# Selective attention and SwiGLU in one kernel: the last 64 queries of batch 0 among the feed-forward products, its causal mask by a matmul, single PSUM banks, loads one behind another

## The chip, the cores and the metric

The kernel runs on one core of one Trainium2 chip. The metric is the time of one execution on the device in microseconds, here 382.61 as the median of three runs (382.60 to 382.98). The profile that is read below is of one further execution of 383.17 us, whose span from the first to the last instruction is 381.3 us.

## The reference: what is computed

Attention with a positional bias over 8 batches, 8 heads, 576 positions and head width 64, and then a SwiGLU feed-forward block over the 4608 tokens that come out of it (width 512, inner width 1536). All inputs are float32.

```python
scores = q @ k.T / sqrt(64)
cum    = cumsum(maximum(s, 0))                      # per batch and head
bias   = -(cum[:, None] - cum[None, :])
scores = where(causal, -1e9, scores + minimum(bias, 0))
attn   = softmax(scores)                            # rows end at the diagonal
x      = (attn @ v) as [tokens, heads * 64]
out    = (silu(x @ w_gate) * (x @ w_val)) @ w_out
```

576 positions are four blocks of 128 and a tail of 64. The 4608 tokens are nine feed-forward tiles of 512, so a tile isn't a batch: tile 0 needs the first 512 queries of batch 0 and no more.

## The kernel before

All products are in bf16. A score product takes k as the stationary operand and q as the moving one, so a block of scores has keys on the partitions; the bias is in it by four further rows of both operands (the tile HL, copied by small transfers into kq). The exponential writes bf16 into `pt`; the causal triangle is then set to zero by an affine select on GpSimd; the product with v (with a column of ones for the sum) gives the output and its divisor; four or five transposes per pair of heads bring it into `XT`, from which the feed-forward tiles read. All instructions of an engine run in the order in which the program lists them. Batch 0's attention runs ahead of everything (`first_batch`), and the attention of the later batches is pumped in small pieces among the feed-forward products.

The parts that matter here; `take` gives the PSUM bank that was released longest ago:

```python
    CHUNKS = [
        [(0, 0, 128), (1, 128, 256), (2, 256, 384), (3, 384, 512)],
        [(0, 128, 576), (3, 512, 576)],
        [(1, 256, 576), (2, 384, 576)],
        [(4, 512, 576)],
    ]
    CHUNK_PT = [1088, 576, 0, 512]
# ... (cut)
        bank = {}
        for i in range(2):
            bank["w", i] = psa.tile([128, 1024], FP32, name=f"wide{i}")
        for i in range(4):
            bank["s", i] = psa.tile([128, 512], FP32, name=f"one{i}")
        released = {key: i - 8 for i, key in enumerate(bank)}
        clock = [0]
        OPEN = 1 << 40

        def take(kind="s"):
            b = min((x for x in bank if x[0] == kind), key=lambda x: released[x])
            assert released[b] < OPEN
            released[b] = OPEN
            return b

        def give(b):
            clock[0] += 1
            released[b] = clock[0]
# ... (cut)
        def score_piece(bh, ci):
            hb, hh = divmod(bh, HB)
            pair = bh < H
            if ci == 0:
                pts[bh] = PTP[0].tile(
                [128, PTW], BF16, tag="pt", bufs=PTP["bufs"], name="pt"
            )
            pt = pts[bh]
            r, e = divmod(hh, 2)
            T = KQ[hb % 2][r]
            if pair:
                if ci % 2 == 0:
                    bs = take("w")
                    scs[bh] = bs
                else:
                    bs = scs[bh]
                base = (512, 0, 0, 512)[ci]
            else:
                bs = take()
                base = 0
            o = base
            n = sum(hi - lo for _, lo, hi in CHUNKS[ci])
            sc = view(bs, 1024 if pair else 512)
            for (tj, lo, hi) in CHUNKS[ci]:
                w = hi - lo
                nc.tensor.matmul(
                    sc[:, o : o + w],
                    T[:, 1, e * S + 128 * tj : e * S + 128 * (tj + 1)],
                    T[:, 0, e * S + lo : e * S + hi],
                    start=True,
                    stop=True,
                )
                o += w
            if not pair or ci % 2 == 1:
                if pair:
                    c0, W = ((576, 1024), (0, 576))[ci // 2]
                else:
                    c0, W = CHUNK_PT[ci], n
                nc.scalar.activation(pt[:, c0 : c0 + W], sc[:, 0:W], AF.Exp, scale=0.125)
                give(bs)
            if ci == (1 if pair else 0):
                nc.gpsimd.affine_select(
                    pt[:, 1088:1600], pt[:, 1088:1600], pattern=[[0, 4], [1, 128]],
                    compare_op=ALU.is_ge, fill=zreg, base=0, channel_multiplier=-1,
                )
            if ci == 3:
                nc.gpsimd.affine_select(
                    pt[:, 512:576], pt[:, 512:576], pattern=[[1, 64]],
                    compare_op=ALU.is_ge, fill=zreg, base=0, channel_multiplier=-1,
                )
# ... (cut)
        def gate_value(tt, hps, sus):
            xt = XT[:, :, (tt % 3) * TT : (tt % 3 + 1) * TT]
            for ft in range(NFT):
                j, f0 = divmod(ft * 128, WCH)
                gbs = take()
                pg = view(gbs, TT)
                for c in range(4):
                    nc.tensor.matmul(
                        pg, WG[j][:, c, f0 : f0 + 128], xt[:, c, :],
                        start=(c == 0), stop=(c == 3),
                    )
                th = hpool.tile([128, TT], BF16, tag="th", name="th")
                nc.scalar.activation(th, pg, AF.Tanh, scale=0.5)
                pp = hpool.tile([128, TT], BF16, tag="pp", name="pp")
                nc.vector.scalar_tensor_tensor(
                    pp, in0=th, scalar=1.0, in1=pg, op0=ALU.add, op1=ALU.mult
                )
                give(gbs)
                yield 1.0
# ... (cut)
        cast_half(0, "k", 0, nc.scalar)
        cast_half(0, "q", 0, nc.scalar)
        aug(0, SP4)
        load_v(0, range(5))
        load_qk(2)
        for nm in ("k", "q"):
            for g in range(2):
                pe_transpose_half(0, nm, g, 0)
        pe_out(0, "k", 0, 0, nc.scalar)
        pe_out(0, "k", 1, 0, nc.scalar)
        pe_out(0, "q", 0, 0, nc.vector)
        pe_out(0, "q", 1, 0, nc.vector)
        cast_half(0, "k", 1, nc.scalar)
        cast_half(0, "q", 1, nc.gpsimd)
        aug(1, GP4)
        for nm, eng in (("k", nc.scalar), ("q", nc.vector)):
            for g in range(2):
                pe_transpose_half(0, nm, g, 1)
                pe_out(0, nm, g, 1, eng)
        cast_one(1, "k", nc.vector)
        cast_one(1, "q", nc.vector)
# ... (cut)
        def first_batch():
            wq = {1: (("g", 0), ("v", 0)), 4: (("g", 1),), 5: (("v", 1),)}
            tail = {
                6: ("a0", "a1"),
                7: ("a2", "a3", "a4", "x0", "a5", "x1", "a6", "a7", "x2", "w6", "x3", "w8"),
            }
            for h in range(H):
                for ci in range(4):
                    score_piece(h, ci)
                for w in wq.get(h, ()):
                    w_load(*w)
                if h == 1:
                    order = [(nm, g) for g in range(2) for nm in ("k", "q")]
                    for nm, g in order:
                        pe_transpose(1, nm, g)
                    for r in range(2):
                        for nm, g in order:
                            pe_out(1, nm, g, r, nc.vector)
                    for c in range(3, 5):
                        cast_v(0, c, nc.vector)
                if h == 2:
                    for c in range(3):
                        cast_v(0, c, nc.gpsimd)
                if h == 3:
                    aug(2, SP4)
                if h == 7:
                    aug(3, SP4)
                    load_qk(3)
                    load_v(1, range(5))
                    load_qk(4)
                    cast_one(2, "k", nc.gpsimd)
                    cast_one(2, "q", nc.gpsimd)
                    load_qk(5)
                    w_load("o", 0)
                    w_load("o", 1)
                for what in tail.get(h, ()):
                    i = int(what[1:])
                    if what[0] == "a":
                        av_piece(i, range(NCH))
                        av_out(i)
                    elif what[0] == "x":
                        x_pe(i, nc.scalar)
                    else:
                        keep_warm(i)

        first_batch()
        second_psum()
# ... (cut)
        hook = {
            1: [lambda: prep_one(2, 0)],
            2: [lambda: prep_one(2, 1)],
            3: [lambda: prep_one(2, 2)],
            4: [lambda: prep_one(2, 3)],
            6: [lambda: cast_one(3, "k", nc.gpsimd), lambda: cast_one(3, "q", nc.gpsimd)],
        }
        for tt in range(NTT):
            lo = H * (tt + 1) + LAGS[tt]
            hi = min(H * (tt + 2) + LAGS[tt + 1], BH + 2)
            span = 36 if tt < FIRST7 else 34.5
            if hi == BH + 2:
                span = 30
            n0 = 6 if tt == 0 else 0
            n = 0
            todo = {FIRST7 - 1: W_SUMS, FIRST7: W_DIFFS}.get(tt, [])
            for i, cost in enumerate(ffn_items(tt)):
                n += cost
                if todo and (i >= 24 if tt < FIRST7 else i % 4 == 2):
                    weight_op(*todo.pop(0))
                if i >= 2 * NFT or i % 4 == 1:
                    do_later(1)
                for f in hook.pop(n, ()):
                    f()
                pump(lo + (hi - lo) * min(1.0, max(0, n - n0) / (span - n0)))
```

The softmax here doesn't subtract the row's maximum and nothing guards it: scores larger than these inputs give would overflow.

## Time and profile before

| What | Value |
|---|---|
| median time | 382.61 us (3 runs, 382.60 to 382.98) |
| span in the profile | 381.3 us, 8674 instructions |
| VectorE, ScalarE, GpSimd busy | 289.6, 242.7 and 205.9 us |
| gate and value products, 128x512, x432 each | 110.9 and 110.8 us busy |
| tanh on ScalarE, 128x512, x108 | 64.7 us, 599 ns each |
| select 128x512 and 128x64 on GpSimd, x64 each | 41.8 and 16.7 us, 653 and 261 ns each |
| DMA, whole run | 64.22 MB in 100729 packets, 81888 of them under 512 B |

In the tables of the profile "busy" counts pipelined matmuls by modelled ends, so two successive busy times can overlap: four products of 512 columns are shown as 1.03 us, while the next group begins 0.86 us after them. "L375" is line 375 of the kernel file, "[0.57 <-DMA ...]" an idle time of the engine and what ended it.

### The profile page before, as it was taken

The page shows a single profiled execution, that of the slowest core. Times are in us where ns is not written, and L with a number is a line of the kernel's source. Part 1 is how long each engine was busy: PE and PEld are TensorE (multiplying, and loading weights), DVE is VectorE, ACT ScalarE, POOL GpSimd, SP SyncE. Part 2 cuts the span into 40 slices and gives each one's busy share as a digit, 9 for nine tenths or more (in the row PEclk, how much of TensorE's full clock was granted, in tenths as well). Part 3 has the DMA queues.
Part 4 walks back from the last instruction along what each step waited for, and adds up shares of the span by engine and source line. Part 5 has one row for each costly group of instructions (what it writes and reads, how often), then busy time and mean ns, then how long its engine had stood idle before and what let it go on. Part 6 is the DMA issues. An engine that isn't in the chain of part 4 may idle for free. (4 is left out here: it accounts for less than half of the span.)

```text
span 381.3 us, 8674 instructions
## 1 busy us (share of the span) xinstructions
PE 363.5 (95%) x3246; PEld 230.5 (60%) x3246; DVE 289.6 (76%) x577; ACT 242.7 (64%) x459; POOL 205.9 (54%) x326
## 2 busy tenths in 40 slices
PE   3779999998999999999999999999999999999995
PEld 3666556655555555865586558655875575476464
DVE  8666787456895799868986899589958866975983
ACT  8586788676977786578767876697455523323321
POOL 6684357545364636595458647775665426315220
PEclk9999999999999999999999999999999999999999
DMA  7999999997477998498739965987223213002003
GB/s 234 197 253 263 198 242 268 348 259 162 163 167 246 236 285 220 105 287 216 194 114 285 270 149 158 252 179 166 37 80 101 32 19 127 0 2 97 14 2 110
DMA packets 100729, 64.22 MB, mean 168 GB/s; under 512 B 81888, under 2 KB 85824, under 8 KB 100688
## 3 DMA queue, kind: packets, MB, share of 16 engines
q1 hardware_dynamic: 91248, 46.15, 48.6%
q0 software_dynamic: 9440, 17.53, 17.7%
q8 instruction: 25, 0.41, 0.4%
q14 instruction: 16, 0.13, 0.1%
HBM read 37.90 MB, written 19.86 MB: 151 GB/s over the span
## 5 line engine op out<-in xcount | busy, mean ns | idle before, releaser
L388 ACT ACTIVATE pt<-bank 128x512 bf16<-128x512 f32 x224 | 106.7, 506 | 26.5 <-PE bank L375 18.3
L626 PE MATMUL bank<-XT,wg 128*128 128x512 bf16 x432 | 110.9, 379 | 0.6 <-DVE pp L633 0.2
L641 PE MATMUL bank<-XT,wv 128*128 128x512 bf16 x432 | 110.8, 379 | 0.2
L631 ACT ACTIVATE th<-bank 128x512 bf16<-128x512 f32 x108 | 64.7, 599 | 60.0 <-PE bank L626 54.7
L633 DVE SCALAR_TENSOR_TENSOR pp<-th,bank 128x512 bf16<-128x512 bf16 x108 | 73.9, 684 | 30.2 <-ACT th L631 29.5
L649 DVE SCALAR_TENSOR_TENSOR ht<-pp,bank 128x512 bf16<-128x512 bf16 x108 | 74.1, 686 | 10.3 <-POOL ht L658 0.5
L658 POOL TENSOR_TENSOR ht<-ht 128x512 bf16<-128x512 bf16 x35 | 40.4, 1154 | 53.9 <-DVE su L656 53.8
L375 PE MATMUL bank<-kq 128*128 128x128 bf16 (+4 forms) x504 | 67.5, 240 | 1.6 <-DVE kq L284 1.1
L375 PEld LDWEIGHTS <-kq 128*128 128x128 bf16 x576 | 46.7, 99 | 34.8 <-issue 5.7
L641 PEld LDWEIGHTS <-wv 128*128 128x128 bf16 x432 | 38.6, 98 | 35.8 <-issue 0.4
L626 PEld LDWEIGHTS <-wg 128*128 128x128 bf16 x432 | 38.5, 98 | 35.2 <-issue 1.2
L391 POOL TENSOR_SCALAR_AFFINE_SELECT pt<-pt 128x512 bf16<-128x512 bf16 x64 | 41.8, 653 | 28.5 <-ACT pt L388 28.1
L413 PEld LDWEIGHTS <-pt 128*128 128x128 bf16 x960 | 41.1, 98 | 16.0
L413 PE MATMUL bank<-vt,pt 128*128 128x65 bf16 x840 | 41.8, 194 | 0.0
L447 POOL DMA_DIRECT2D xs<-ot x24 | 21.9, 912 | 31.7 <-DVE ot L430 31.7
L711 PEld LDWEIGHTS <-ht 128*128 128x128 bf16 x336 | 31.2, 98 | 4.3
L197 POOL DMA_DIRECT2D kq<-HL x52 | 31.2, 602 | 0.1
L430 DVE TENSOR_TENSOR ot<-bank,rc 128x320 bf16<-128x320 f32 x56 | 27.5, 492 | 1.9
L396 POOL TENSOR_SCALAR_AFFINE_SELECT pt<-pt 128x64 bf16<-128x64 bf16 x64 | 16.7, 261 | 18.9 <-ACT pt L388 18.7
L711 PEld LDWEIGHTS <-su 128*128 128x128 bf16 x252 | 23.6, 98 | 3.3
L670 PE MATMUL bank<-wo,ht 128*128 128x512 bf16 x96 | 24.6, 379 | 0.0
L775 POOL TENSOR_TENSOR ysb<-ysb 128x512 f32<-128x512 f32 x12 | 15.2, 1271 | 15.3 <-DVE ysb L770 15.3
(96 smaller groups left out, 396.9 us busy)
## 6 DMA issues: line engine op xcount, KB each, us to landing
rawk<-in_k_dram SPq DMA_DIRECT2D x15, 576.0 KB
rawq<-in_q_dram SPq DMA_DIRECT2D x15, 576.0 KB
rawv<-in_v_dram SPq DMA_DIRECT2D x32, 256.0 KB
out_dram<-ysb POOLq DMA_DIRECT2D x32, 256.0 KB, 3.8
xs<-ot POOLq DMA_DIRECT2D x24, 160.0 KB, 3.7
ks<-ck SPq DMA_DIRECT2D x11, 288.0 KB
qs<-cq SPq DMA_DIRECT2D x11, 288.0 KB
wg<-in_moe_w_gate_dram POOLq DMA_DIRECT2D x2, 768.0 KB, 12.6
```

The source lines that it names most:

```text
L197: engs[hh].dma_start(KQ[hb % 2][r][r0 : r0 + 4, :, e * S : (e + 1) * S], HL[bh : bh + 1, :, :, :],)
L375: nc.tensor.matmul(sc[:, o : o + w], T[:, 1, e * S + 128 * tj : e * S + 128 * (tj + 1)], T[:, 0, e * S + lo : e * S + hi], start=True, sto ...
L388: nc.scalar.activation(pt[:, c0 : c0 + W], sc[:, 0:W], AF.Exp, scale=0.125)
L391: nc.gpsimd.affine_select(pt[:, 1088:1600], pt[:, 1088:1600], pattern=[[0, 4], [1, 128]], compare_op=ALU.is_ge, fill=zreg, base=0, channel ...
L413: nc.tensor.matmul(av[:, bi * (D + 1) : (bi + 1) * (D + 1)], pt[:, c0 : c0 + 128], VT[b % 2][:, tj, h, :], start=(tj == 0), stop=(tj == bi),)
L626: nc.tensor.matmul(pg, WG[j][:, c, f0 : f0 + 128], xt[:, c, :], start=(c == 0), stop=(c == 3),)
L631: nc.scalar.activation(th, pg, AF.Tanh, scale=0.5)
L633: nc.vector.scalar_tensor_tensor(pp, in0=th, scalar=1.0, in1=pg, op0=ALU.add, op1=ALU.mult)
L641: nc.tensor.matmul(pv, WV[j][:, c, f0 : f0 + 128], xt[:, c, :], start=(c == 0), stop=(c == 3),)
L649: nc.vector.scalar_tensor_tensor(hp[:, 2 * k2 : 2 * k2 + 2, :].rearrange("p a n -> p (a n)"), in0=pp, scalar=0.5, in1=pv, op0=ALU.mult, op ...
L658: (nc.vector if ft == NFT - 1 else nc.gpsimd).tensor_sub(hp[:, 1:3, :], hp[:, 1:4:2, :], hp[:, 0:3:2, :])
L711: nc.tensor.matmul(ps, lhs(p), rhs(p), start=(first and p == 0), stop=(last and p == NP - 1), skip_group_check=True,)
```

## The change

Four things are changed at the start of the kernel.

1. **Last 64 queries later.** Batch 0's prologue (`score_first`, `av_first`, `x_first`) handles queries 0 to 511 only. Queries 512 to 575 get functions of their own (`score_tail`, `av_tail`, `x_tail`), which are called by hooks among the units of feed-forward tile 0. This is for letting tile 0 begin with what it needs. Batch 1's attention, which began after unit 6 of tile 0, now begins after unit 12.
2. **Mask by a matmul.** For the 512 diagonal columns of a head a first product with the identity writes a triangle of -32768 into the bank, and the score products add to it. The exponential then gives zeros there, so that the selects of GpSimd in the prologue are not needed.
3. **Single banks.** The two pairs of wide banks of the prologue are gone; eight single banks serve the whole kernel. One of them is held for filler products that keep TensorE busy in the prologue. Two gate groups are begun with three of their four products before the last pair of heads is in `XT`.
4. **Loads in a line.** Most of v of batch 0, the q and k of head blocks 2 and 3, and the weights are issued from GpSimd in the order of their use; the output weights come later, in units 14 and 17 of tile 0.

Some casts change engine as well: k of head block 1 from VectorE to ScalarE, q of head block 1 from VectorE to GpSimd, and v of batch 0 all to GpSimd; a memset of 64x1216 moves from VectorE to GpSimd, and two small ones for v from GpSimd to VectorE.

The core of the diff:

```diff
+        def score_first(bh, cs=(0, 1, 2)):
+            hb, hh = divmod(bh, HB)
+            if cs[0] == 0:
+                pts[bh] = PTP[0].tile([128, 1280], BF16, tag="pt", bufs=8, name="pt")
+            r, e = divmod(hh, 2)
+            T = KQ[hb % 2][r]
+            for ci in cs:
+                c0, blocks = FIRST_CHUNKS[ci]
+                bs = take()
+                o = 0
+                if ci == 0:
+                    nc.tensor.matmul(
+                        view(bs, 512), ident, lower, start=True, stop=False,
+                        skip_group_check=True,
+                    )
+                for (tj, lo, hi) in blocks:
+                    nc.tensor.matmul(
+                        bank[bs][:, o : o + hi - lo],
+                        T[:, 1, e * S + 128 * tj : e * S + 128 * (tj + 1)],
+                        T[:, 0, e * S + lo : e * S + hi],
+                        start=(ci > 0),
+                        stop=True,
+                        skip_group_check=(ci == 0),
+                    )
+                    o += hi - lo
+                nc.scalar.activation(
+                    pts[bh][:, c0 : c0 + o], view(bs, o), AF.Exp, scale=0.125
+                )
+                give(bs)
 ... (cut)
+        def score_tail(bh):
+            hb, hh = divmod(bh, HB)
+            pr, e2 = divmod(bh, 2)
+            if e2 == 0:
+                tls[pr] = PTP[0].tile([128, 3, TT // 2], BF16, tag="su", bufs=NFT // 2, name="su")
+            r, e = divmod(hh, 2)
+            T = KQ[hb % 2][r]
+            bs = take()
+            sc = view(bs, NCH * 64)
+            for tj in range(NCH):
+                nc.tensor.matmul(
+                    sc[:, tj * 64 : (tj + 1) * 64],
+                    T[:, 1, e * S + 128 * tj : e * S + 128 * (tj + 1)],
+                    T[:, 0, e * S + 512 : e * S + S],
+                    start=True,
+                    stop=True,
+                )
+            tl = tail_view(pr)
+            nc.scalar.activation(
+                tl[:, e2].rearrange("p c n -> p (c n)"), sc, AF.Exp, scale=0.125
+            )
+            give(bs)
+            if e2 == 1:
+                nc.gpsimd.affine_select(
+                    tl[:, :, 4, :], tl[:, :, 4, :], pattern=[[0, 2], [1, 64]],
+                    compare_op=ALU.is_ge, fill=zreg, base=0, channel_multiplier=-1,
+                )
+
 ... (cut)
+        spare = take()
+
+        def keep_warm(n):
+            for _ in range(n):
+                nc.tensor.matmul(view(spare, 128), ident, ident, start=True, stop=True)
+
+        keep_warm(32)
         cast_half(0, "k", 0, nc.scalar)
         cast_half(0, "q", 0, nc.scalar)
-        aug(0, SP4)
-        load_v(0, range(5))
-        load_qk(2)
+        load_v(0, (0, 1), nc.gpsimd)
         for nm in ("k", "q"):
             for g in range(2):
                 pe_transpose_half(0, nm, g, 0)
@@ -861,74 +1001,67 @@
         pe_out(0, "k", 1, 0, nc.scalar)
         pe_out(0, "q", 0, 0, nc.vector)
         pe_out(0, "q", 1, 0, nc.vector)
+        aug(0, SP4)
+        aug(1, SP4)
+        load_v(0, (4,))
         cast_half(0, "k", 1, nc.scalar)
         cast_half(0, "q", 1, nc.gpsimd)
-        aug(1, GP4)
+        load_v(0, (2, 3), nc.gpsimd)
+        w_load("g", 0)
         for nm, eng in (("k", nc.scalar), ("q", nc.vector)):
+            keep_warm(10)
             for g in range(2):
                 pe_transpose_half(0, nm, g, 1)
                 pe_out(0, nm, g, 1, eng)
-        cast_one(1, "k", nc.vector)
-        cast_one(1, "q", nc.vector)
-
-        def keep_warm(n):
-            bs = take()
-            for _ in range(n):
-                nc.tensor.matmul(
-                    view(bs, 128), ident, ident, start=True, stop=True
-                )
-            give(bs)
-
-        ... (first_batch, shown above, is cut)
+        keep_warm(10)
+        cast_one(1, "k", nc.scalar)
+        cast_one(1, "q", nc.gpsimd)
+        w_load("v", 0)
+        for c in range(4):
+            cast_v(0, c, nc.gpsimd)
+
+        def half_batch(nm):
+            for g in range(2):
+                pe_transpose(1, nm, g)
+                pe_out(1, nm, g, 0, nc.vector)
+
+        score_first(0)
+        half_batch("k")
+        score_first(1)
+        half_batch("q")
+        for nm in ("k", "q"):
+            for g in range(2):
+                pe_out(1, nm, g, 1, nc.vector)
+        for nm in ("k", "q"):
+            load_one(2, nm, eng=nc.gpsimd)
+        score_first(2)
+        score_first(3)
+        w_load("g", 1)
+        score_first(4)
+        av_first(0)
+        w_load("v", 1)
+        score_first(5)
+        av_first(1)
+        av_first(2)
+        for nm in ("k", "q"):
+            load_one(3, nm, eng=nc.gpsimd)
+        score_first(6)
+        av_first(3)
+        av_first(4)
+        score_first(7)
+        cast_v(0, 4, nc.gpsimd)
+        av_first(5)
+        x_first(0)
+        av_first(6)
+        x_first(1)
+        x_first(2, nc.vector)
+        av_first(7)
+        for ft in range(2):
+            products("g", ft, XT[:, :, 0:TT], range(3))
+        x_first(3)
+        give(spare)
         first_sbuf.close()
 ... (cut)
-        hook = {
-            1: [lambda: prep_one(2, 0)],
-            2: [lambda: prep_one(2, 1)],
-            3: [lambda: prep_one(2, 2)],
-            4: [lambda: prep_one(2, 3)],
-            6: [lambda: cast_one(3, "k", nc.gpsimd), lambda: cast_one(3, "q", nc.gpsimd)],
-        }
+        hook = {n: [] for n in range(1, 37)}
+        for bh in range(H):
+            hook[1 + bh].append(lambda bh=bh: score_tail(bh))
+        hook[4].append(lambda: aug(2, SP4))
+        hook[5].append(lambda: cast_one(2, "k", nc.gpsimd))
+        hook[6].append(lambda: av_tail(0))
+        hook[6].append(lambda: cast_one(2, "q", nc.gpsimd))
+        hook[8].append(lambda: aug(3, SP4))
+        hook[8].append(lambda: load_v(1, range(5)))
+        hook[9].append(lambda: init_vt(1, nc.gpsimd))
+        hook[10].append(lambda: av_tail(1))
+        hook[12].append(x_tail)
+        for i in range(4):
+            hook[8 + i].append(lambda i=i: prep_one(2, i))
+        hook[14].append(lambda: w_load("o", 0))
+        hook[14].append(lambda: [cast_one(3, nm, nc.gpsimd) for nm in ("k", "q")])
+        hook[15].append(lambda: load_qk(4))
+        hook[17].append(lambda: w_load("o", 1))
+        hook[20].append(lambda: load_qk(5))
         for tt in range(NTT):
             lo = H * (tt + 1) + LAGS[tt]
             hi = min(H * (tt + 2) + LAGS[tt + 1], BH + 2)
             span = 36 if tt < FIRST7 else 34.5
             if hi == BH + 2:
                 span = 30
-            n0 = 6 if tt == 0 else 0
+            n0 = 12 if tt == 0 else 0
```

## The prediction

> **What bounds the kernel now.** I read three views in this order: the shares and slices of the page, a table of stages, and the order of time of single engines at the start. The page first:
>
> ```profile
> PE 363.5 (95%) x3246; PEld 230.5 (60%) x3246; DVE 289.6 (76%) x577; ACT 242.7 (64%) x459; POOL 205.9 (54%) x326
> ...
> PE   3779999998999999999999999999999999999995
> ```
>
> TensorE is busy 95% of 381.3 us, and its row is low only in the first three slices (9.5 us each) and the last one. The chain that ended last is almost empty in this page (three lines of 0%), so it can't be used here. The stretch table says the same in microseconds (the columns after the length are busy times of PE, PEld, DVE, ACT, POOL with their counts, then clock, DMA share, GB/s):
>
> ```profile
> 0.00:10.00 10.00, 3.88 (x33) 3.40 (x34) 7.69 (x12) 8.14 (x11) 7.10 (x19) 1.00 0.72 237
> 10.00:20.00 10.00, 7.22 (x60) 5.68 (x59) 7.45 (x11) 5.96 (x9) 6.72 (x14) 1.00 0.96 209
> 20.00:30.00 10.00, 8.42 (x171) 7.18 (x170) 6.41 (x18) 8.08 (x11) 8.92 (x17) 1.00 1.15 234
> 30.00:40.00 10.00, 9.64 (x77) 5.62 (x77) 6.60 (x12) 6.51 (x11) 3.40 (x4) 1.00 1.12 258
> 60.00:100.00 40.00, 38.90 (x398) 23.42 (x397) 24.95 (x51) 31.12 (x58) 20.79 (x39) 1.00 0.91 243
> 340.00:382.00 42.00, 36.64 (x242) 23.42 (x240) 26.98 (x53) 11.16 (x21) 10.39 (x11) 1.00 0.14 51
> ```
>
> In 30 us TensorE loses 6.1 + 2.8 + 1.6 = 10.5 us; between 30 and 340 us about 2.5; at the end about 4.6. So the run is a prologue (batch 0's attention), then a TensorE-bound body, then an end that the change doesn't touch. The order of time on TensorE shows where the body begins, and what the prologue's rhythm is:
>
> ```profile
> 11.15 1.51 PE L375 MATMUL wide<-kq 128*128 128x128 bf16 x9 [0.57 <-DMA kq<-HL]
> ...
> 18.34 0.95 PE L375 MATMUL wide<-kq 128*128 128x128 bf16 x9 [0.86 <-ACT pt L388]
> 20.05 0.95 PE L375 MATMUL wide<-kq 128*128 128x128 bf16 x9 [0.77 <-ACT pt L388]
> ...
> 32.03 1.02 PE L626 MATMUL bank<-XT,wg 128*128 128x512 bf16 x4 [0.17 <-ACT XT L468]
> ```
>
> The first feed-forward product starts at 32.03. A head takes 1.71 us (18.34 to 20.05), of which TensorE waits 0.77: there are only two pairs of wide banks, and the exponentials must empty one before it is written again. ScalarE and VectorE in the same stretch:
>
> ```profile
> 17.26 10.13 ACT L388 ACTIVATE pt<-wide 128x1024 bf16<-128x1024 f32 x12 [1.35 <-PE wide L375]
> ```
> ```profile
> 15.43 5.63 DVE L326 COPY kq<-one 64x640 bf16<-64x640 bf16 x8 [2.30 <-ACT pt L388]
> ```
>
> Twelve exponentials (six heads) fill 10.13 us without a gap: 1.69 us a head, so ScalarE sets the prologue. The costs of one instruction:
>
> ```profile
> L388 ACT ACTIVATE pt<-wide 128x1024 bf16<-128x1024 f32 x8 | 8.2, 1024 | 4.6 <-PE wide L375 3.9
> L388 ACT ACTIVATE pt<-bank 128x512 bf16<-128x512 f32 x168 | 96.5, 598 | 26.5 <-PE bank L375 18.3 <-issue 6.9 <-DVE ot L430 0.4
> ```
>
> **What the Trainium skill says.** (1) "ScalarE: Activation LUTs", Rules for kernel authors: about 0.3 us for each ACTIVATE plus about 0.83 ns an element. The trace agrees on the slope, (1024 - 598) / 512 = 0.83 ns, but not on the constant: 598 - 512 x 0.83 = 173 ns. I use the trace's. (2) "TensorE: Matmul & The Clock Gate", What's actually happening: the array runs at half clock until it has been busy for some 3.4 us. The trace agrees by durations: nine score products of a head took 1.51 us at 11.15 and 0.95 from 18.34 on. (The granted-clock row shows full speed throughout, so that row is no help.) (3) "DMA: Bandwidth & Descriptors", Queues, rings and completion order: each DMA engine goes round between the queues that have work. The trace fits: from 20 to 24 us the GpSimd queue took 75.7% and the sync queue 36.1% of the engines at once. So a load issued from GpSimd competes with those of the sync queue. (4) The same page, Specifications: transfers under 512 B don't reach line rate. Agrees: from 12 to 16 us, with 3413 of 3419 packets under 512 B (v has rows of 256 B), 217 GB/s moved at a share above 100%, while up to 438 GB/s moved just after 8 us with longer rows.
>
> **The change part by part.**
>
> *Start of the exponentials.* Before, the first one starts at 12.22: the score products waited for the bias rows (kq from HL) until 11.15, and ran cold. The change takes a VectorE memset of 1.07 us out of the way of the bias rows and puts two small ones in its place, and warms the array with 32 products from about 1.5 us on (at the cold 0.13 us each until about 5.5, when the first cast ends). But ScalarE now also casts k of head block 1 (1.15 us, its row of 128x1152 casts) ahead of its first exponential: its copies ended at 10.2 before, so this ends at about 11.4 if the load is there, and the load of v from GpSimd may compete with it. Estimate: first exponential at 11.9, 0.3 us won.
>
> *Exponentials.* Each head now has 1280 columns without the last 64 queries, in pieces of 512, 512 and 256, where it had 1024 and 576. In the order of time two 512s back to back take 1.09 us, so one costs 0.49 to the next; one of 256 is 0.173 + 256 x 0.83 ns = 0.385 alone, less the same overlap of 0.11, 0.28. Sum 1.26 us a head, 10.1 us for eight, against 12.22 to 27.39 = 15.2 before: up to 5.1 won. On the other side TensorE gets a mask product per head (512 columns at 0.215 us, from four of them in 0.86): 8 x 0.215 = 1.7 us, which lies in the time in which it waited. GpSimd loses 8 + 8 selects (8 x (0.65 + 0.26) = 7.3 us), which were beside the path except the last.
>
> *What stops the exponentials from running through.* VectorE still splits q and k of head block 1: eight copies, 5.63 us. The order of instructions shows that they come k then q for the first half, and k then q for the second, and the banks of the transposes come free only with the second half, while heads 3 and 4 need those banks. The q ones need a cast on GpSimd that stands behind four v loads (nearer 1 us each, by 0.91 of the like-sized xs store) and one weight load (0.78): about 13.5 to 14.6 us. Then copies end at about 18.5 to 19.5, and head 4 starts its exponentials at 19.0 to 19.9 instead of 17. I book 2.2 us of stall: exponentials end at 11.9 + 10.1 + 2.2 + 0.3 for joints = 24.5 against 27.39.
>
> *From the last exponential to the body.* Before 32.03 - 27.39 = 4.64 us (two heads' products with v, three pairs' transposes and copies in turn, 14 filler products). Now only head 7's products with v (10 at 31 ns = 0.3), reciprocal and multiply (0.65), four transposes (0.3) and a copy (0.6) remain, with six real gate products (6 x 0.215 = 1.3) in their midst: about 2.4 us, 1.3 of it body work. So the body's equivalent start is 24.5 + 2.4 - 1.3 = 25.6: 6.4 us earlier than 32.03.
>
> *Given back in the body.* The tail of batch 0 is not saved but moved there, where TensorE is the bound: 40 score products of 64 columns and 40 products with v at about 30 ns (fifteen take 0.46 us in the trace), and 4 small transposes: 2.5 us. Batch 1's attention is pumped over 24 units of tile 0 in place of 30, so ScalarE (31.12 of 40 us between 60 and 100) gets denser; I book 0.7 us of new gaps.
>
> Sum: 382.6 - 6.4 + 2.5 + 0.7 = 379.4.
>
> **Rivals.** *ScalarE runs through* (banks free in time): the 2.2 us stall goes, 377.2. For: seven banks are in rotation instead of two pairs; against: the VectorE copies stand in order and can't be passed. *Loads become the bound*: gate weights are needed at about 24.5 us, and about 2.45 MB of q, k and s, 1.25 MB of v and 0.77 MB of weights must land before. From 24 to 28 us the trace moves 212 GB/s with weights, and v 217; that gives v by 16 and the gate weights by about 19 to 20, the value weights by 23. Slack of 3 to 4 us; if v's small rows from GpSimd are slower, the body waits and the time is 382 to 386. *Tile 0 gets ScalarE-bound*, or the output weights, now issued at units 14 and 17 where they took 19.5 us to land before, are late for unit 24: 2 to 4 us lost, 381.5 to 383.5. For: GpSimd and sync queues share the engines, share 0.91 there; against: at least 10 us between issue and need. *The body takes all back*: only if its present gaps are needed as slack; against: PE at 38.90 of 40 with waits of 1.1 us at most.
>
> **Range and chances.** The gain of the prologue is sure in sign (less ScalarE work, fewer handovers), with 4.5 to 8.5 us; the price of 2.5 to 6 us is nearly sure too. Hence 375.8 to 384.0. For 2% it would need 375.0, which wants the run-through and no new gap: 0.07. Slower by 2% (390.3) needs two of the waits of the rivals at once: 0.04.
>
> **What would show it.** Right: the first L771 (tanh) product group (gate) at 23.5 to 26 us, eight heads' exponentials (L375 of the changed file) ending near 24.5, VectorE copies into kq ending near 19, and TensorE's busy total in the body up by 2 to 3 us, with gaps there about as before. Wrong: gate products waiting for wg by DMA; the exponentials waiting for TensorE longer than 3 us in sum; or ScalarE named in front of products between 40 and 75 us.

## The result: 387.05 us, and the profile after

| | before | after |
|---|---|---|
| median time | 382.61 us (4 runs, 382.44 to 382.98) | 387.05 us (4 runs, 386.74 to 387.83) |
| ratio to before | | 1.0118, 95% interval 1.0100 to 1.0135 |
| span in the profile | 381.3 us | 385.0 us |
| first feed-forward product | 32.03 us | 26.26 us |
| first product of tile 1 | 79.81 us | 83.41 us |

The change makes the kernel slower by 1.2%. The prediction was 379.4 with a range up to 384.0, so it was wrong, in size and in sign. The page of the changed kernel (busy totals, TensorE's row, the granted clock's row; a slice is 9.6 us):

```profile
PE 367.1 (95%) x3326; PEld 232.4 (60%) x3326; DVE 288.7 (75%) x579; ACT 243.7 (63%) x476; POOL 207.9 (54%) x322
...
PE   6689979998999999999999999999999999999994
...
PEclk9999998999999999999999999999999999999999
```

The first slices are fuller than before (668 where there was 377). But the sixth slice has a 7, and the seventh digit of the clock's row is an 8. Both lie in tile 0. Stretches of the changed kernel (columns as in the table of the prediction: length, busy PE, PEld, DVE, ACT, POOL, granted clock, DMA share, GB/s):

```profile
0.00:10.00 10.00, 6.73 (x79) 5.86 (x79) 7.72 (x13) 8.21 (x11) 8.97 (x20) 1.00 0.77 255
10.00:20.00 10.00, 6.33 (x70) 4.62 (x71) 7.09 (x11) 6.56 (x14) 9.89 (x15) 1.00 1.03 202
20.00:30.00 10.00, 9.21 (x144) 6.77 (x143) 5.03 (x18) 7.48 (x17) 1.78 (x3) 1.00 1.12 266
30.00:40.00 10.00, 10.00 (x121) 6.13 (x119) 6.72 (x12) 6.57 (x14) 4.10 (x8) 1.00 0.93 243
50.00:55.00 5.00, 4.62 (x41) 2.85 (x40) 2.73 (x4) 4.62 (x10) 2.84 (x7) 1.00 1.10 159
55.00:60.00 5.00, 2.54 (x15) 1.29 (x15) 4.16 (x7) 2.64 (x6) 4.89 (x10) 0.90 0.98 160
60.00:65.00 5.00, 5.00 (x51) 2.87 (x50) 2.56 (x6) 2.29 (x5) 3.21 (x5) 0.76 1.07 287
```

Between 55 and 60 us TensorE works 2.54 of 5 us. In the kernel before it worked all 5 there, at clock 1.00:

```profile
55.00:60.00 5.00, 5.00 (x59) 3.11 (x57) 3.63 (x8) 3.26 (x7) 4.99 (x10) 1.00 1.03 400
```

From 60 to 65 us the changed kernel's TensorE is fully busy, but at clock 0.76. From tile 1 on nothing more is lost: it begins 3.6 us later than before, and the last tile 3.4 us later (349.99 against 346.58). So the whole loss is made between the first product at 26.26 and tile 1 at 83.41. This stretch is the length of tile 0, and most readings below are of it.

**The start.** TensorE in order of time (start, length, what was done, and in brackets the idle time and what ended it):

```profile
13.08 0.73 PE L366 MATMUL bank<-kq 128*128 128x128 bf16 x7 [1.44 <-DMA kq<-HL]
...
17.88 0.38 PE L361 MATMUL bank<-lower,ident 128*128 128x512 bf16 x1 [1.41 <-DVE kq L317]
...
26.26 1.68 PE L757 MATMUL bank<-XT,wg 128*128 128x512 bf16 x6
...
28.84 0.38 PE L757 MATMUL bank<-XT,wg 128*128 128x512 bf16 x1 [0.67 <-ACT XT L416]
```

The score products wait for the bias rows until 13.08, where they began at 11.15 before. The six products that are begun early run from 26.26 to 27.78; the next follows at 28.84. Without that gap the body would have begun at 28.84 - 1.52 = 27.3. ScalarE in the same stretch:

```profile
13.52 3.92 ACT L375 ACTIVATE pt<-bank 128x512 bf16<-128x512 f32 x9 [2.26 <-PE bank L366]
18.51 1.41 ACT L375 ACTIVATE pt<-bank 128x512 bf16<-128x512 f32 x3 [1.08 <-PE bank L366]
20.50 5.18 ACT L375 ACTIVATE pt<-bank 128x512 bf16<-128x512 f32 x12 [0.58 <-PE bank L366]
```

Nine exponentials are three heads: 3.92 / 3 = 1.31 us a head. Two stalls follow, 1.08 + 0.58 = 1.66 us, and the last one ends at 20.50 + 5.18 = 25.7.

**Tile 0.** A unit, by which the hooks count, is one step of a tile; tile 0 has 36 of them: 12 gate groups, 12 value groups and 12 steps of the output layer. TensorE's two long waits, and the products after them:

```profile
55.91 0.38 PE L288 MATMUL bank<-ident,cq 128*128 128x128 bf16 x4 [1.29 <-DVE kq L317]
57.84 0.38 PE L506 MATMUL bank<-kq 128*128 128x128 bf16 x4 [1.55 <-DVE kq L317]
...
58.93 1.87 PE L757 MATMUL bank<-XT,wg 128*128 128x512 bf16 x4
```

A transpose and a score product (L288, L506) wait for VectorE's copies out of the banks of earlier transposes (L317). Line 317 is the split of q of head block 3 into `kq`. Why VectorE is late there is seen on ScalarE and VectorE themselves:

```profile
50.84 1.50 ACT L315 COPY kq<-bank 64x640 bf16<-64x640 bf16 x2
52.36 0.71 ACT L515 ACTIVATE pt<-bank 128x512 bf16<-128x512 f32 x2
52.96 0.60 ACT L771 ACTIVATE th<-bank 128x512 bf16<-128x512 f32 x1
```
```profile
53.60 0.69 DVE L773 SCALAR_TENSOR_TENSOR pp<-th,bank 128x512 bf16<-128x512 bf16 x1 [2.17 <-ACT th L771]
54.20 1.65 DVE L317 COPY kq<-bank 64x640 bf16<-64x640 bf16 x2
```

The tanh at 52.96 belongs to a gate group that TensorE had done by 51.53 (its group began at 50.67, and one takes 0.86). It stood in ScalarE's line behind two copies (1.50 us) and two exponentials. VectorE had nothing else in front of it and stood idle for 2.17 us; then its copies came late, and TensorE, whose transposes need their banks, stood too. VectorE had time to spare (busy 2.73 of the 5 us from 50 on). ScalarE had none: it was busy 4.62 of these 5 us, and from 50.34 to 57.09 it ran without a gap. So the crowd of some 7 us is on ScalarE, and the order of the lines passes its delay on to VectorE and from there to TensorE.

The granted clock, one microsecond at a time:

```profile
55.00:56.00 1.00, 0.09 (x2) 0.09 (x2) 0.95 (x3) 0.97 (x3) 1.00 (x3) 1.00 1.09 158
57.00:58.00 1.00, 0.15 (x3) 0.15 (x3) 0.97 (x3) 0.09 (x1) 0.89 (x3) 1.00 1.07 176
...
60.00:61.00 1.00, 1.00 (x4) 0.34 (x3) 0.00 (x0) 0.10 (x1) 0.86 (x2) 0.50 1.26 281
...
62.00:63.00 1.00, 1.00 (x11) 0.49 (x10) 0.21 (x1) 0.59 (x2) 0.35 (x2) 0.81 0.78 224
```

From 55 to 58 TensorE is busy 0.09 + 0.29 + 0.15 = 0.53 us. From about 59.0 to 62.4 it runs at 0.50 of full speed: four products take 1.66 us (58.93 to 60.59) in place of 0.86. The lost speed adds up to 0.02 + 0.50 + 0.50 + 0.50 + 0.19 = 1.7 us.

**The sum.** The body starts 32.03 - 27.3 = 4.7 us earlier. The tail's products cost 3.0 us there: eight groups of scores at 0.15, two groups with v at 0.75, transposes 0.25. Waits cost 1.29 + 1.55, 0.61 at the tail's transposes and, by the starting times, 0.18 ahead of batch 1's first score product: 3.6. The kernel before had 0.4 us of waits in its tile 0 (0.20 and 0.22), so 3.2 are new. The clock costs 1.7. -4.7 + 3.0 + 3.2 + 1.7 = +3.2; the spans differ by 3.7, so 0.5 us stays unassigned. The 4.7 holds for these two executions: that of late_before (below), with the prologue of the kernel before, began its body at 29.93.

### The profile page after: what moved, and what is told of

Same layout as the page of the kernel before. It is cut to its first block, busy times and chain, and to the rows that moved or that the text cites. A ratio compares the mean times of both kernels' runs of the same rounds, so it can differ in the third digit from the quotient of the medians.

```text
span 385.0 us, 8871 instructions
## 1 busy us (share of the span) xinstructions
PE 367.1 (95%) x3326; PEld 232.4 (60%) x3326; DVE 288.7 (75%) x579; ACT 243.7 (63%) x476; POOL 207.9 (54%) x322
## 5 line engine op out<-in xcount | busy, mean ns | idle before, releaser
L757 PE MATMUL bank<-XT,wg 128*128 128x512 bf16 x432 | 112.1, 381 | 0.8 <-ACT XT L416 0.7
L506 PE MATMUL bank<-kq 128*128 128x128 bf16 (+4 forms) x504 | 67.9, 241 | 3.0 <-DVE kq L317 1.6
L506 PEld LDWEIGHTS <-kq 128*128 128x128 bf16 x504 | 40.8, 98 | 29.9 <-issue 3.4
L518 POOL TENSOR_SCALAR_AFFINE_SELECT pt<-pt 128x512 bf16<-128x512 bf16 x56 | 36.6, 654 | 30.9 <-ACT pt L515 30.6
L540 PEld LDWEIGHTS <-pt 128*128 128x128 bf16 x840 | 37.0, 98 | 15.8
L183 POOL DMA_DIRECT2D kq<-HL x48 | 28.7, 599 | 0.1
L523 POOL TENSOR_SCALAR_AFFINE_SELECT pt<-pt 128x64 bf16<-128x64 bf16 x56 | 14.6, 261 | 18.2 <-ACT pt L515 18.1
```

The lines of the kernel that those rows point to most:

```text
L183: engs[hh].dma_start(KQ[hb % 2][r][r0 : r0 + 4, :, e * S : (e + 1) * S], HL[bh : bh + 1, :, :, :],)
L506: nc.tensor.matmul(sc[:, o : o + w], T[:, 1, e * S + 128 * tj : e * S + 128 * (tj + 1)], T[:, 0, e * S + lo : e * S + hi], start=True, sto ...
L518: nc.gpsimd.affine_select(pt[:, 1088:1600], pt[:, 1088:1600], pattern=[[0, 4], [1, 128]], compare_op=ALU.is_ge, fill=zreg, base=0, channel ...
L540: nc.tensor.matmul(av[:, bi * (D + 1) : (bi + 1) * (D + 1)], pt[:, c0 : c0 + 128], VT[b % 2][:, tj, h, :], start=(tj == 0), stop=(tj == bi),)
L757: nc.tensor.matmul(view(bs, TT), w[:, c, f0 : f0 + 128], xt[:, c, :], start=(c == 0), stop=(c == 3),)
```

## The experiments

Unless the heading says otherwise the edit is to the changed kernel. In the table "tile 0" is the time from the first feed-forward product to the first product of tile 1 in the profiled run. It is 1.06 us longer in all kernels with the change's prologue, by the gap after the six products. The last three columns are of one execution, which need not lie at the median (v_late's took 384.77 us, best3's 383.70). Ratios are to the kernel before on the same chip (382.79 to 382.99 there).

| kernel | median us | ratio, 95% interval | first product | tile 1 | tile 0 |
|---|---|---|---|---|---|
| before | 382.61 | | 32.03 | 79.81 | 47.78 |
| after | 387.05 | 1.0118 (1.0100 to 1.0135) | 26.26 | 83.41 | 57.15 |
| dense_before | 386.89 | 1.0087 (1.0057 to 1.0118) | 32.34 | 84.09 | 51.75 |
| late_before | 383.68 | 1.0028 (1.0004 to 1.0052) | 29.93 | 80.37 | 50.44 |
| no_tails | 384.76 | 1.0036 (1.0019 to 1.0053) | 25.58 | 80.19 | 54.61 |
| v_late | 385.65 | 1.0063 (1.0043 to 1.0084) | 24.30 | 81.68 | 57.38 |
| hl_free | 387.73 | 1.0120 (1.0096 to 1.0144) | 28.79 | 84.49 | 55.70 |
| select_mask | 387.68 | 1.0124 (1.0091 to 1.0157) | 27.21 | 84.23 | 57.02 |
| spread | 396.54 | 1.0348 (1.0312 to 1.0384) | 28.35 | 92.95 | 64.60 |
| prep_early | 386.70 | 1.0092 (1.0058 to 1.0125) | 26.09 | 82.82 | 56.73 |
| prep_spread | 386.34 | 1.0090 (1.0065 to 1.0114) | 26.17 | 82.08 | 55.91 |
| both_fixed | 385.69 | 1.0070 (1.0042 to 1.0098) | 26.29 | 82.51 | 56.22 |
| best1 | 384.33 | 1.0044 (1.0024 to 1.0065) | 24.98 | 80.30 | 55.32 |
| best2 | 387.06 | 1.0108 (1.0077 to 1.0139) | 24.35 | 83.38 | 59.03 |
| best1_load5 | 383.13 | 0.9996 (0.9983 to 1.0010) | 25.26 | 80.08 | 54.82 |
| both_load5 | 384.43 | 1.0034 (1.0021 to 1.0047) | 25.80 | 81.64 | 55.84 |
| after_load5 | 386.17 | 1.0087 (1.0066 to 1.0108) | 26.56 | 83.93 | 57.37 |
| best3_wo | 383.72 | 1.0019 (1.0002 to 1.0036) | 26.02 | 80.42 | 54.40 |
| best3 | 384.90 | 1.0049 (1.0033 to 1.0064) | 26.05 | 80.37 | 54.32 |
| best1_load5k | 382.75 | 0.9991 (0.9974 to 1.0007) | 25.34 | 79.35 | 54.01 |

### Is it the crowd in tile 0?

**dense_before**: the kernel before, its prologue untouched, with only the schedule of tile 0 that the change uses. Besides the hooks this moves the transposes of head block 3 (`PREP_AT`), a part of the change that the diff above leaves out.

```diff
-            2: {(0, 3): 0, (1, 3): 1, (2, 1): 2, (2, 3): 3},
+            2: {(2, 1): 0, (2, 3): 1, (3, 1): 2, (3, 3): 3},
-            1: ... 4: prep_one(2, 0..3),  6: cast_one(3, ...)
+            8: ... 11: prep_one(2, 0..3), 14: cast_one(3, ...)
-            n0 = 6 if tt == 0 else 0
+            n0 = 12 if tt == 0 else 0
```

> The kernel before, with batch 1's attention begun at unit 12 of tile 0 instead of 6, and the preparation of head blocks 2 and 3 moved as the change moves it; no tails, old prologue, old loads. Theory 'crowding' (the dense stretch makes TensorE wait for VectorE's copies of head block 3, and the waits let its clock drop): 386 to 388 us, waits of TensorE for kq copies between 55 and 65 us, a granted clock below 1 there. Rival 'tails' (the added tail work is what costs): 382.3 to 383.5 us, no such waits.

Measured 386.89: a loss about as large as the change's (the intervals overlap), without its prologue and without a tail in tile 0. TensorE in order of time:

```profile
46.14 0.85 PE L375 MATMUL bank<-kq 128*128 128x128 bf16 x9 [1.41 <-DVE kq L326]
...
58.04 0.38 PE L297 MATMUL bank<-ident,cq 128*128 128x128 bf16 x4 [1.29 <-DVE kq L326]
59.98 0.38 PE L375 MATMUL bank<-kq 128*128 128x128 bf16 x4 [1.56 <-DVE kq L326]
```

Lines 297, 326 and 375 of the old file are 288, 317 and 506 of the new one. The two waits of the changed kernel are there to within a hundredth, and an earlier one: 4.3 us in all, where tile 0 is 4.0 us longer than before. So the waits belong to the new schedule of tile 0. The clock, which was expected below 1, stays at 1.00 here.

**late_before**: the kernel before with the `PREP_AT` line alone.

> The kernel before with one edit: head block 3 prepared at the changed kernel's places, attention still begun at unit 6. 'Straight ahead of its reader': the two waits of 1.3 and 1.6 us appear although the stretch is no denser, 384.5 to 387 us. 'Density': no new waits, 382.5 to 383.3 us.

383.68, between the two expectations. One wait of 1.46 us (a score product at 51.91, for the same copies) shows that this line alone makes such a stall. The time rises by 0.9 us, and the rest of dense_before's loss is left to the later beginning of batch 1 and the later transposes of block 2, which were not run one by one. (Its profiled run began the body 2.1 us earlier than the kernel before although its prologue is the same: its first nine score products took 1.14 us, where those of the kernel before took 1.51. TensorE then had to wait 0.65 us for the value weights, so its length of tile 0 is no measure.)

**no_tails**: the calls of the tail's functions are left out, with the tail's products, exponentials and transposes; `XT[:, :, 512:576]` is set to zero instead.

```diff
-            hook[1 + bh].append(lambda bh=bh: score_tail(bh))
-        hook[6].append(lambda: av_tail(0))
-        hook[10].append(lambda: av_tail(1))
-        hook[12].append(x_tail)
+        nc.gpsimd.memset(XT[:, :, 512:576], 0.0)
```

> The changed kernel without the tails: score_tail, av_tail and x_tail are left out, and the 64 columns of XT that they fill are set to zero; all else is as changed. Theory 'crowding': only the tails' own 3 us and the 0.6 us wait at their end go, the waits near 55 us and the slow clock stay: 383 to 384.5 us. Rival 'tails': the waits go as well, 377.5 to 380 us.

384.76, 2.3 us less than the change, and tile 0 is 2.5 us shorter. The waits of 1.29 and 1.55 stay (at 52.55 and 54.49), and the clock falls after them as well (0.72 from 55 to 60). The wait of 0.61 us at the tail's transposes is gone, but in its place stands one of 1.41, as in dense_before:

```profile
40.66 0.85 PE L507 MATMUL bank<-kq 128*128 128x128 bf16 x9 [1.41 <-DVE kq L318]
```

So the 2.5 us are a difference: 3.0 of products and 0.6 of waiting go, and about 1.4 of other waiting comes. The tail does not make the long waits.

### The start

**v_late**: v's first two loads behind GpSimd's cast of q of block 0, the next two behind its cast of q of block 1.

```diff
-        load_v(0, (0, 1), nc.gpsimd)
... (cut)
-        load_v(0, (4,))
... (cut)
         cast_half(0, "q", 1, nc.gpsimd)
-        load_v(0, (2, 3), nc.gpsimd)
-        w_load("g", 0)
+        load_v(0, (0, 1), nc.gpsimd)
+        load_v(0, (4,))
... (cut)
         cast_one(1, "q", nc.gpsimd)
+        load_v(0, (2, 3), nc.gpsimd)
+        w_load("g", 0)
```

> The changed kernel with v's first two loads issued by GpSimd behind its cast of q (about 9.4 us instead of 7.3) and the other two behind its cast of q of head block 1. If v's loads hold the bias rows up on the shared DMA engines: the bias rows land by 11.5 to 12.2 us, no wait of TensorE for them over 0.6 us, first exponential 1 to 1.6 us earlier than 13.5, time 385.3 to 386.3 us. If it is the later issue of the bias rows alone (8.77 us): they still land near 13 us and the time stays at 386.7 to 387.5.

The bias rows, 9 KB for each head, now come in time. The scores of the first and of the second head in v_late:

```profile
10.88 0.71 PE L366 MATMUL bank<-kq 128*128 128x128 bf16 x7
...
12.47 0.73 PE L366 MATMUL bank<-kq 128*128 128x128 bf16 x7 [0.17 <-DMA kq<-HL]
```

The first head, which had waited 1.44 us and begun at 13.08, begins at 10.88 without a wait; the second waits 0.17 us for its own rows. The first product comes at 24.30, 2.0 us earlier, and the run is 1.4 us shorter. From 9 to 13 us GpSimd's queue had taken 74.6% of the DMA engines and the sync queue, with the bias rows, 21.8%; in v_late it is 45.4 and 18.0%. So v's small rows from GpSimd delay the bias rows, and most of what the prologue failed to win is this. Not every execution shows all of it: nine of the traces here have these loads; three of them begin the body at 24.30 to 24.98, and six, whose clock falls at the start (last section), at 25.26 to 26.29.

**hl_free**: the memset of 64x1216 that the change had moved to GpSimd goes back to VectorE, behind its bias chain and its copies of block 0; the bias rows of block 1 and v's last load follow it.

```diff
-        nc.gpsimd.memset(aug_rows(1, 0), 0.0)
-        aug(1, SP4)
-        load_v(0, (4,))
... (cut)
+        nc.vector.memset(aug_rows(1, 0), 0.0)     # behind the q copies
... (cut)
+        aug(1, SP4)
+        load_v(0, (4,))
```

> The changed kernel with the 64x1216 memset of head block 1 moved from GpSimd at the start to VectorE behind its copies, where it idles; the bias rows of head block 1 follow it. If GpSimd's memsets slow VectorE's steps that make the bias rows (cast 1.25 us against 0.83 before, copy 0.84 against 0.45) and so delay the first exponential: bias rows complete near 7.9 instead of 8.7 us, the first exponential 0.5 to 0.9 us earlier, time 386.0 to 386.6. If the loads of v, not this, hold the bias rows up: the first exponential stays at 13.5 or is up to 0.5 us later, since v's loads are issued earlier too, and the time stays at 386.7 to 387.5.

A miss that helps. The bias chain on VectorE ended 1.1 us earlier (7.16 + 0.45 = 7.6 against 8.7), but GpSimd was free earlier too and issued v at 5.98 instead of 7.34; the wait for the bias rows rose to 3.39 us, the clock fell to 0.50 from 14 to 17 us, and the time didn't fall. Issued at 7.7 instead of 8.8, the rows released the scores at 14.14 instead of 13.08. So the chain is not what holds them up: what lies in the DMA queues when they are issued is.

**select_mask**: GpSimd's select again in place of the mask product.

```diff
-                    nc.tensor.matmul(view(bs, 512), ident, lower, start=True, stop=False, ...)
+                    nc.gpsimd.affine_select(pts[bh][:, 0:512], ..., fill=zreg, ...)
```

> The changed kernel with the mask of the prologue by a select on GpSimd (128x512, 0.65 us a head) behind the first exponential of each head, and no mask product. If the mask product is worth what it was made for (GpSimd has loads and casts to issue in the same stretch): the products with v wait for selects behind GpSimd's loads, weights are issued up to 5 us later, gate products start 0.5 to 2 us later, 387.3 to 389 us. If it only trades hidden work for hidden work: 386.5 to 387.3 us.

387.68 lies in the range of the first theory but is not told apart from the change: the intervals overlap. The first product comes 1.0 us later, but the wait for the bias rows happened to be 2.40 instead of 1.44, which is the same 1.0. The products with v wait for a select once, 0.45 us. The mask product is thus worth nothing that these runs can show.

### Moving the crowd

**spread**: tails two to a unit, transposes of block 2 at units 3 to 6, batch 1 from unit 7, the transposes of block 3 early.

```diff
-            hook[1 + bh].append(lambda bh=bh: score_tail(bh))
+            hook[1 + bh // 2].append(lambda bh=bh: score_tail(bh))
-            hook[8 + i].append(lambda i=i: prep_one(2, i))
+            hook[3 + i].append(lambda i=i: prep_one(2, i))
-            n0 = 12 if tt == 0 else 0
+            n0 = 7 if tt == 0 else 0
... (cut: the casts, the second halves of the tail and PREP_AT are moved forward too)
```

> The changed kernel with the tails two to a unit (units 1 to 4), head block 2 prepared in units 3 to 6, and batch 1's attention begun at unit 7 instead of 12, head block 3 prepared from its fifth head on. Theory 'crowding': the waits near 55 us and the slow clock go (2.8 + 1.7 us), 381.5 to 383.5 us. Rival 'tails': the same work is packed even closer, 386 to 389 us.

396.54, the worst of all. Everything comes earlier except the loads: TensorE waits 4.07 us for GpSimd's cast of k and 3.33 us for k itself, whose loads lie where they lay. So this schedule can't be moved forward without its loads.

**prep_early** (block 3's transposes two pieces earlier), **prep_spread** (those of the kernel before, and casts of block 3 at unit 10) and **both_fixed** (prep_early with v_late):

```diff
-            2: {(2, 1): 0, (2, 3): 1, (3, 1): 2, (3, 3): 3},
+            2: {(1, 3): 0, (2, 1): 1, (2, 3): 2, (3, 1): 3},    # prep_early, both_fixed
+            2: {(0, 3): 0, (1, 3): 1, (2, 1): 2, (2, 3): 3},    # prep_spread
```

> The changed kernel with one edit: head block 3 is prepared two pieces of score products earlier (from the end of the tenth head of batch 1's attention count on, the last part two pieces ahead of its reader and not straight ahead of it). Theory 'straight ahead of its reader' (scores of the first head of block 3 stand right behind the last copy that they read, so TensorE waits out that copy): the wait of 1.55 us before L506 goes, the one of 1.29 us before the transposes shrinks, the clock holds, 382.5 to 384.5 us. Theory 'density' (ScalarE and VectorE have too much in units 12 to 24 wherever it stands): the waits turn up elsewhere, 386 to 387.5 us.

> The changed kernel with head block 3 prepared at the places of the kernel before (spread over two heads, the last one a whole head ahead of its reader), and for that its two casts issued at unit 10 instead of 14; attention still begins at unit 12. Theory 'ScalarE's queue' (in the changed kernel the four preparation pieces of 0.75 us copies fall into 1.6 heads and fill ScalarE, 3.95 of 4.00 us from 52 to 56, so the tanh, then VectorE, then TensorE come late): both waits near 55 us go, the clock holds, 382.3 to 384 us. Theory 'density alone' (24 units in place of 30 are too few wherever the preparation stands): waits of 1.5 us or more stay, 385.5 to 387 us.

> The changed kernel with the edits of prep_early and v_late together. If both theories hold and the gains add: 387.05 - 3 to 4.5 (waits and clock) - 1 to 1.6 (start) = 381 to 383 us, at or below the kernel before. If a stall of tile 0 takes up what the start wins: 383 to 384.5 us.

386.70, 386.34 and 385.69: by the medians the first two win 0.4 and 0.7 us, but their intervals overlap the change's, and both_fixed wins no more than v_late alone. Part of that is seen at its start: the granted clock falls to 0.50 from 19 to 22 us, and the first product comes at 26.29 where v_late had 24.30; its tile 0 is 1.2 us shorter than v_late's. prep_early turns the two waits into four (0.42, 0.21, 0.32, 1.70). In prep_spread the two waits shrink to 0.46 and 0.33 and the clock stays at 1.00, but 10 us later comes a new one. ScalarE, then TensorE, in prep_spread:

```profile
65.32 1.15 ACT L245 CAST ck<-rawk 128x1152 bf16<-128x1152 f32 x1 [3.10 <-DMA rawk<-in_k_dram]
```
```profile
67.02 1.02 PE L805 MATMUL bank<-wo,ht 128*128 128x512 bf16 x4 [1.59 <-ACT pt L515]
```

ScalarE stands 3.10 us before its cast of k of head block 5, until the load lands; the exponentials behind that cast come late, and TensorE lacks a bank.

**best1** (prep_spread, v_late, and the tail's transposes one unit later) and **best2** (prep_spread and v_late with block 2's transposes at units 5 to 8, batch 1 from unit 9, the loads of blocks 4 and 5 two units earlier):

> prep_spread with v's loads as in v_late and the tail's transposes one unit later. If the stall and the start were the two wrong terms: 387.05 - 4.5 - 1.4 - 0.6 = 380.5, so 379.5 to 382 us, faster than before. If density alone stalls: 384 to 386 us.

> As prep_spread with v_late, and head block 2 prepared in units 5 to 8 between the tails instead of 8 to 11 (its casts at units 2 and 3), batch 1's attention begun at unit 9 (27 units instead of 24), loads of head blocks 4 and 5 two units earlier. If density matters at all: 0.5 to 1.5 us below best1, 378.5 to 381 us. If the tails' and the preparation's work collide instead, or the casts wait for their loads: 381 to 385 us with waits between 28 and 42 us.

384.33 and 387.06: neither reaches its first theory, and best2 lies above both of its ranges. Both meet the same wait: ScalarE stands 2.34 us for k of block 5 in best1 (its cast begins at 63.54), and 5.75 us in best2.

### The load behind the load

Why is that load late? It is asked for in unit 20, but issued only at 58.01. The waits of the sync queue between 25 and 80 us in best1 (us in all, times, longest):

```profile
SPq L157 <- POOL pt L523: 11.2, 1, 11.2
```

Line 157 is a load of v: that of batch 2 goes into the same buffer as batch 1's, and so the queue stands for 11.2 us until GpSimd has cast that one, from 54.10 to 56.93 (the profile names the select that ends just after the casts). The queue takes its loads in order, and the load of block 5 is behind it. (The changed kernel shows 11.5 us at the same place, and issues the load at 58.61.)

**best1_load5**, **both_load5** and **after_load5** put the load of block 5 ahead of batch 2's v:

```diff
-        hook[15].append(lambda: load_qk(4))
+        hook[15].append(lambda: [load_qk(4), load_qk(5)])
-        hook[20].append(lambda: load_qk(5))
```

> Kernel: best1 with the load of k and q of head block 5 asked for together with that of block 4, ahead of batch 2's v on the sync queue (in best1 it stood behind v from 43 to 58 us, and ScalarE waited 2.34 us for it before its cast at 63.54). Theory that this late load takes the gain back: ScalarE's wait for it goes, the TensorE wait of 0.83 us near 65 goes with it, tile 1 starts at 79 to 79.7 instead of 80.3, and the time is 383.0 to 383.9 (best1: 384.33). Rival, that the five loads asked for at once compete and other waits turn up, or that TensorE's waits near 65 have another cause: tile 1 at 80 to 81 and 384 to 385.

> Kernel: both_fixed (v loads later at the start, block 2's transposes from unit 0 of tile 0) with the load of head block 5 ahead of batch 2's v. There the two fixes together won no more than one of them (385.69, tile 1 at 82.51), and ScalarE waited 1.20 us for this load. Theory of the late load: tile 1 starts at 81 to 81.8 and the time is 384.2 to 385.2. Rival, that the density of the work of batch 1 in 24 units alone makes the waits: unchanged, 385.3 to 386.2.

> Kernel: the change itself with only the load of head block 5 moved ahead of batch 2's v. A control: in the changed kernel ScalarE reached the cast of block 5 at 65.72 without a wait, since it was already held up by the two waits of TensorE near 56 and 58. Theory (the load binds only once those waits are gone): unchanged, 386.5 to 387.6, tile 1 at 83.1 to 83.7. Rival, that the load is itself a cause of the loss: 385 to 386.

383.13, 384.43 and 386.17. In best1_load5 ScalarE's wait of 2.34 us is gone, and TensorE's of 0.83 and 0.26 us near 65 with it: 1.2 us won, as the late load would have it, though tile 1 starts at 80.08 and not before 79.7: the start lost some clock (last section). both_load5 wins 1.3 us. (The waits of both_fixed are as told above: it moves block 3's transposes, not block 2's.) The control lies between its two ranges, 0.9 us below the change by the median, with an interval that overlaps the change's; in its profile the two waits of 1.29 and 1.55 are as they were, and tile 1 starts at 83.93. All this fits a load that is a second barrier, met mainly when the first is gone, which would be why the first repairs won so little. The control alone doesn't decide it.

**best3_wo** asks for the output weights at units 11 and 13 in place of 14 and 17; **best3** also puts block 2's transposes at units 7 to 10. Both start from best1_load5.

```diff
-        hook[14].append(lambda: w_load("o", 0))
-        hook[17].append(lambda: w_load("o", 1))
+        hook[11].append(lambda: w_load("o", 0))
+        hook[13].append(lambda: w_load("o", 1))
-            hook[8 + i].append(lambda i=i: prep_one(2, i))       # best3
+            hook[7 + i].append(lambda i=i: prep_one(2, i))
```

> Kernel: best1_load5 with the two loads of the output weights asked for at units 11 and 13 of tile 0 in place of 14 and 17 (in best1_load5 the first product of the last feed-forward layer waited 0.64 us for them at 62.12). Theory that loads asked for late are what is left near 62 us: this wait goes, nothing takes its place, 382.3 to 383.0 (best1_load5: 383.13). Rival, that the loads of blocks 4 and 5 then land later in turn and ScalarE waits for them again: 383.1 to 384.2.

> Kernel: best3_wo with the four transposes of head block 2 at units 7 to 10 in place of 8 to 11, so that VectorE's copies of them end before batch 1's first score products (in best1_load5 those waited 0.91 us for a copy into kq at 42.94). Theory that the wait is only a matter of order: it goes, 381.4 to 382.3, level with or just under the kernel before (382.99 on this chip). Rival, that the casts of block 2 on GpSimd then come too late for the transposes and TensorE waits for those instead: 382.3 to 383.5.

383.72 and 384.90, misses both; best3_wo isn't told apart from best1_load5, whose interval overlaps. In best3 the wait of 0.91 goes, but one of 0.65 comes at 50.76. The weights were issued at 42 instead of 45.4 and 49.9, but in best3_wo took 14.2 and 19.9 us to land instead of 12.2 to 12.6, so the second half of them lands at 62.6, where it had landed at 62.5, and TensorE waits for them at the same place (0.43 and, in best3, 1.56 us, at 62.6). From 42 to 62 us the k and q of blocks 4 and 5, the output weights and the rest of batch 1's v go over the engines at once.

**best1_load5k** therefore takes bytes out of that stretch: of block 5 only k goes ahead, and q (0.59 MB) stays behind v.

```diff
-        hook[15].append(lambda: [load_qk(4), load_qk(5)])
+        hook[15].append(lambda: [load_qk(4), load_one(5, "k")])
+        hook[20].append(lambda: load_one(5, "q"))
```

> Kernel: best1_load5 with only k of head block 5 ahead of batch 2's v; its q (0.59 MB) stays behind, to be needed some 4.6 us later than k. Theory that the DMA engines have become the limit between 44 and 62 us (in best3_wo the output weights, asked for 3 to 7 us earlier, landed at the same time): with 0.59 MB less in flight the output weights land about 2 us earlier, the wait of 0.64 us near 62 goes, and the time is 382.2 to 382.9 (best1_load5: 383.13). Rival, that q of block 5 then lands too late behind v and ScalarE waits for it: 383.2 to 384.2.

382.75, ratio 0.9991. The time from issue to landing of the output weights, in best1_load5 and in best1_load5k (us, least, median, most):

```profile
DMA to landing us min/median/max: 12.2/12.4/12.6
```
```profile
DMA to landing us min/median/max: 8.9/9.2/9.6
```

They land 3 us sooner, TensorE no longer waits for them, and ScalarE doesn't wait for q. The 0.4 us under best1_load5 lie within the intervals. This kernel keeps the four parts of the change, with v asked for later and block 3's transposes where they stood before, and takes 4.3 us less than the change; it is level with the kernel before, and not shown to be faster.

## Why the prediction was wrong

*Start of the exponentials* (11.9 predicted, 13.52 measured): wrong. The step took a memset and a cold array for what was in the way. It did name v from GpSimd as a competitor, but booked nothing for it; v_late, whose first exponential starts at 11.30, shows that this alone is worth 1.4 us of the run.

*Exponentials* (1.26 us a head, 2.2 us of stall, end 24.5): right. 1.31 us, 1.66 us of stall behind VectorE's eight copies, which end at 19.8; with the late start the end is 25.7. The rival "ScalarE runs through" falls. That the selects' replacement lies in waiting time fits select_mask. (The prediction set aside the 0.3 us per ACTIVATE of the Trainium skill, "ScalarE: Activation LUTs", Rules for kernel authors, for the trace's 173 ns; it left out that the page gives this figure for a bias read through a pointer.)

*From the last exponential to the body* (2.4 us, of which 1.3 work): right in kind, a bit small. From 25.7 to 28.84 it is 3.2 us, 1.5 of them work. Body at 27.3, not 25.6: 4.7 us won instead of 6.4; 1.2 of the missing 1.7 are the late end of the exponentials.

*The tail in the body* (2.5): right in kind; 3.0 by TensorE's order of time, and no_tails won 2.3 to 2.5.

*"I book 0.7 us of new gaps"*: this is the step that failed. The new waits are 3.2 us, and the clock takes 1.7 more. The reasoning named the right engine, ScalarE, which gets denser when 24 units take the work of 30, but put it down as a share of busy time. What decided was a stretch of 7 us without a gap on ScalarE, and the order in each engine's line: a tanh behind two copies and two exponentials, VectorE idle behind the tanh, TensorE behind VectorE. dense_before has the two waits without the rest of the change; prep_spread, with block 3's copies spread out, has 0.46 and 0.33 us in their place. The links of this chain are read from the trace; no run changed the order of ScalarE's line alone. The rival "tile 0 gets ScalarE-bound, 2 to 4 us lost" had the right place, and for the waits the right size; it left out the clock, and I gave it too little weight. The sign I gave for it, ScalarE named in front of products, was wrong: the profile names VectorE there, and ScalarE one step back. "Output weights late" did not happen in the changed kernel, where other waits came first; it did in best1_load5.

*The clock* was in no step and no rival. The Trainium skill, "TensorE: Matmul & The Clock Gate", What's actually happening, says that the array goes to half clock after an idle window of about 3.4 us, that it takes such a window of sustained work to get the full clock, and that the windows run freely. I had used this only for the cold start. The trace agrees on the length: 0.50 from about 59.0 to 62.4, that is 3.4 us at half speed and 1.7 us lost. It shows also that TensorE need not be idle for this: it did 0.53 us of work from 55 to 58. That windows run freely would explain why dense_before, with 0.40 us of work between 57 and 60, keeps a clock of 1.00; no run here shows where the windows lie.

Sum by its terms: start 1.7 us worse, tail 0.5, gaps 2.5, clock 1.7: 6.4 of the 7.65 us between 379.4 and 387.05. The remainder is the 0.5 us left unassigned above, and 0.7 between spans and times: the profiled run of before, at 383.17, lay above its median, and that of after, at 386.74, below.

## What to carry to other kernels

Work that is moved out of a prologue into a stretch that is already full costs its products there (3.0 us for the tail), and making room for it can cost more: batch 1's attention in 24 units in place of 30 went with 3.2 us of new waits. Follow one unit of that stretch through all engines, and ask for each small item what it stands behind, rather than compare shares of busy time.

When a repair wins less than the wait it removes, look for what is next in line at the same place. Here that was a load held up in an in-order queue by another load's buffer, and behind that the bytes in flight.

## What the runs showed of the hardware

- A few stalls in a row, each under 1.6 us, can cost the clock. In tile 0 of after, no_tails, v_late, select_mask and after_load5 it fell to 0.50 after waits of 1.29 and 1.55 us (0.66 or 0.67 in the worst 5 us); in hl_free and dense_before the same two waits left it at 1.00. In both_fixed, both_load5, best1_load5, best3_wo, best3 and best1_load5k it fell at the start, after the stall behind VectorE's copies at 14 to 18 us: in best1_load5k the clock is 0.50 from 17 to 20 us, about 1.7 us of lost speed. v_late and best1 have the same stall and keep 1.00, so which executions fall is open. It fell after longer waits as well: at the start of hl_free (3.39 us), spread (2.55) and select_mask (2.40), and in best2 after 2.87 us at 66. In no_tails the one execution with a mean clock of 1.000 took 381.9 us, and the twelve with 0.987 to 0.993 took 383.6 to 385.5; but in after the slowest execution, 387.83 us, has the highest mean, 0.996. (The mean counts the end of the run too, where TensorE is idle.)
- TensorE waited up to 3.39 us for bias rows of 9 KB that were issued 1.4 to 1.8 us after GpSimd had asked for v; when v was asked for at 8.96 instead of 7.34, the first head's scores didn't wait, and the second's 0.17.
- VectorE's cast of 64x576 took 1.25 us (after) and 1.49 us (v_late, select_mask) with GpSimd's memset of 64x1216 beside it, and 0.56 us without (hl_free). That the memset is the cause was not tried apart. The copy behind the cast doesn't follow the memset: it took 0.84 us in after, and 0.45 in v_late and hl_free.
